# One transposing transfer for each block of four units, and fewer units turned on TensorE, in the backward loop of an attention and MLP block

## The chip, the cores and the metric

The kernel runs on one core of a Trainium2 chip. Its time is the device time of one execution in microseconds, given as the median of several runs. The engines are named as in the profile: PE is TensorE, PEld its weight load, DVE VectorE, ACT ScalarE, POOL GpSimd, SP SyncE, which here only issues DMAs.

## The reference

A transformer block with adaptive layer norm is run forward, and the gradients of its inputs and weights are computed. There are 2048 tokens, a width of 512, 32 heads of 16 columns each and an MLP of 1792 columns with a squared ReLU.

```
h = layernorm(x) * (1 + ca) + sa
x = x + ga * attention(h, wqkv, wo)
h = layernorm(x) * (1 + cb) + sb
x = x + gb * (relu(h @ w1 + b1)**2 @ w2 + b2)
out, vjp = jax.vjp(f, x, wqkv, wo, w1, b1, w2, b2, c, w_mod)
return out, *vjp(grad_out)
```

The part that matters here is the gradient of attention. With scores S = q k^T / 4, E is exp of the scores, normalised by rows; dP is the product of the output's gradient with v. Then dS = E * (dP - row sums), dV = E^T dO, dK = dS^T q and dQ = dS k. Scores and dS have 2048 x 2048 entries for each head.

## The kernel before

The kernel has three stages. The first makes the forward pass and the gradient of the MLP (to about 1116 us in the profile), the second is the backward loop of attention (to about 2388 us), and the third makes the gradients of the projections and of the norm. The change is in the second alone.

The backward loop goes over 8 groups of four heads (`hg`), four chunks of 512 keys (`kc`), four chunks of 512 queries (`qc`) and four tiles of 128 queries (`qi`). One step of the innermost loop is a *unit*: 128 queries by 512 keys for four heads. Four units with the same `hg`, `kc` and `qc` are a *block*; there are 512 units and 128 blocks. For each unit

- PE makes the scores of the four heads (`score`, L1594) into one of three PSUM banks A, B and C, and ACT takes their exponentials (`expo`, L1600) into `E_u`;
- PE makes dP for two heads at a time (`dp_pair`, L1614), and DVE multiplies by `E_u` (L1616), which gives `dS_u` in bf16, with queries on the partitions;
- PE adds `dS_u` and `E_u` into dK and dV (`k_quad` L1654, `v_quad` L1663), in one accumulator `accVK` for each chunk of keys.

dQ needs dS with the keys on the partitions. So every unit, 128 x 2048 values of 2 bytes, that is 0.5 MB, is turned into the tile `dsT`, in one of two ways. Most units are turned by a transposing DMA from SBUF to SBUF, issued by SP (`transpose_unit`, L1629 and L1631). In every second block (`on_pe`) the fourth unit is turned on TensorE instead (`pe_turn`, L1644, 16 squares of 128 x 128 in two halves into PSUM), and ACT copies the halves into `dsT` (L1760). When a block's `dsT` is whole, PE makes its dQ in 16 products (`dq_quad`, L1681) and ACT scales it out of PSUM (`dq_out`, L1691 or L1694); POOL adds it up over the chunks of keys (L1699).

`dS_u` is held in tiles of two units, of which there are four, and `dsT` in tiles of a block, of which there are three.

The order of instructions on PE, ACT, DVE, SP and POOL is written out by hand. The loop over blocks b walks through one of two lists of tokens: `order_t` in a block whose predecessor has a unit turned on TensorE, `order_n` otherwise. A token `s3` is the score 3 of the 16 of block b, `e3` its exponential, `D` the next dP pair and its dS, `q` the next dK or dV quad, `t1`, `T1`, `t2` and `T2` the two halves of the turn of block b - 1 on PE and their copies on ACT, `d1` and `d2` two dQ quads each of block b - 2, `Q` their way out, and `f`, in `order_t` alone, an extra product of PE (`keep_warm`, L1637). Both lists hold 16 scores, 16 exponentials and 8 D. The D run a little behind: the first D of block b makes the last dS of block b - 1. After a unit's second D the loop calls `transpose_unit`, so the transfers are issued by SP in the order of the units, and each waits there for its dS.

The loads of the next group of heads are issued by ACT within the loop, one for each four D. The loads of the third stage are issued by SP behind the last transfers (from L1778 on).

Of the kernel before, what the change touches and what calls it, by code (L numbers as in the profile page):

```python
# [17 lines left out]
BF = dt.bfloat16  # L18
F32 = dt.float32

P = 128
# [13 lines left out]
def kernel(  # L35
# [21 lines left out]
    SP = nc.sync  # L57
# [89 lines left out]
    with ExitStack() as ph:  # L147
# [4 lines left out]
        ework = att.enter_context(tc.tile_pool(name="phCe", bufs=4))  # L152
# [1393 lines left out]
        SP.dma_start(out=tile_ap, in_=(dQc if key == "dq" else dVKtP)[i])  # L1546

    with ExitStack() as ph:
        tpool = ph.enter_context(tc.tile_pool(name="phIt", bufs=3))
        ework = ph.enter_context(tc.tile_pool(name="phIe", bufs=4))  # L1550
        wk = ph.enter_context(tc.tile_pool(name="phIw", bufs=2))
        psd = ph.enter_context(tc.tile_pool(name="psId", bufs=2, space=bass.MemoryType.PSUM))
# [3 lines left out]
        hst, bst, sst, dqt, cur = {}, {}, {}, {}, {}  # L1556
# [45 lines left out]
        def dp_pair(u, pair):  # L1602
            hg, kc, qc, qi = units[u]
            st = hst[hg]
            qt = qc * 4 + qi
            if pair == 0:
                if qi % 2 == 0:
                    cur["dS"] = ework.tile([P, 2, 4, 512], BF, name="dS_u", tag="dS_u", bufs=4)
                bst[u][1] = cur["dS"][:, qi % 2]
            E_u, dS_u = bst[u]  # L1610
            psD = psd.tile([P, 2, 512], F32, name="psD_u", tag="pd")
            for hi in range(2):
                r = 32 * (2 * pair + hi)
                PE.matmul(psD[:, hi, :], st["do"][r:r + 32, qt * P:(qt + 1) * P], st["v"][r:r + 32, kc * 512:kc * 512 + 512],  # L1614
                          start=True, stop=True, tile_position=(r, 0))
            DVE.tensor_tensor(dS_u[:, 2 * pair:2 * pair + 2, :], psD[:], E_u[:, 2 * pair:2 * pair + 2, :], ALU.mult)  # L1616
            if qi == 3 and on_pe(u // 4):
                held["dS"] = dS_u

        def on_pe(b):  # L1620
            return b % 2 == 1

        def transpose_unit(u):
            hg, kc, qc, qi = units[u]
            if qi == 0:
                dqt[u // 4] = tpool.tile([P, 4, 16, P], BF, name="dsT", tag="dsT")
            if on_pe(u // 4) and qi >= 2:
                if qi == 2:
                    SP.dma_start(out=dqt[u // 4][:, qi], in_=bst[u][1].rearrange("p h k -> p (h k)"), transpose=True)  # L1629
            elif qi % 2 == 1:  # L1630
                SP.dma_start(out=dqt[u // 4][:, qi - 1:qi + 1].rearrange("p u b q -> p (u b) q"),  # L1631
                             in_=cur["dS"].rearrange("p u h k -> p (u h k)"), transpose=True)

        held = {}

# [84 lines left out]
        with tc.manual_schedule(engines={PE.engine, ACT.engine, DVE.engine, SP.engine, POOL.engine}):  # L1720
# [3 lines left out]
            idle = psx.tile([P, 512], F32, name="idle", tag="accVK")  # L1724
            for b in range(NU // 4 + 3):
                toks, bank = order_t if on_pe(b - 1) else order_n
                for tok in toks:
                    c, i = tok[0], int(tok[1:] or 0)
# [11 lines left out]
                    elif c == "D":  # L1740
                        if 0 <= nD < 2 * NU:
                            dp_pair(nD // 2, nD % 2)
                            if nD % 2 == 1:
                                transpose_unit(nD // 2)
                        nD += 1
                        cur["j"] = nD
                        for j in sorted(j for j in todo if j <= nD):
                            for f, args in todo.pop(j):
                                f(*args)
                    elif c == "q":  # L1750
                        if 0 <= nq < 2 * NU:
                            (v_quad if nq % 2 else k_quad)(nq // 2)
                        nq += 1
                    elif c == "f" and 0 < nq < 2 * NU:
                        keep_warm()
                    elif c == "t" and 0 <= b - 1 < NU // 4:
                        pe_turn(b - 1, i - 1)
                    elif c == "T" and 0 <= b - 1 < NU // 4:
                        dst, pt = held.pop(i - 1)
                        ACT.activation(dst, pt[:], AF.Identity)  # L1760
                    elif c == "d" and 0 <= b - 2 < NU // 4:
                        for kt in (2 * i - 2, 2 * i - 1):
                            dq_quad(b - 2, kt)
                    elif c == "Q" and 0 <= b - 2 < NU // 4:
                        dq_out(b - 2)
# [3 lines left out]
    with ExitStack() as ph:  # L1769
# [139 lines left out]
        with tc.manual_schedule(engines={PE.engine, ACT.engine, DVE.engine}):  # L1909
# [33 lines left out]
            for b in range(3):  # L1943
                for ic in range(DC):
# [8 lines left out]
                    elif i <= 2 * DC:  # L1953
                        k, h = (i - 1) // 2, (i - 1) % 2
# [67 lines left out]
```

## Time and profile before

| | |
|---|---|
| median of three runs | 2492.1 us (2487.35 to 2492.11) |
| profiled execution, from its first to its last instruction | 2501.3 us |
| busy: PE, DVE, ACT, POOL | 93%, 73%, 92%, 20% of the span |
| mean granted clock of TensorE | 0.98 |
| backward loop | 1115.7 to 2387.6 us |
| DMA packets | 1189503, of which 1065867 under 512 B |

The profiled execution is one run by itself, with the profiler on; the page gives no other time for it than its span. Busy shares are means over three stages with different limits: in the first stage DVE is busy half of the time, in the loop almost all of it. A row of a timeline has its start in us, its length, engine, line, operation, output and input, and in brackets the idle time before it and what ended that. A row of the chain has start, length and what the chain ran over.

### The profile page before, as it was taken

To read this page: it belongs to the slowest core of one execution; us is meant where nothing else is said; L and a number is where in the kernel's file an instruction comes from. 1 tells how busy PE (TensorE), PEld (TensorE's weight loads), DVE (VectorE), ACT (ScalarE), POOL (GpSimd) and SP (SyncE) were. 2 spreads that over 40 slices of the span, in tenths; PEclk is the share of its full clock that TensorE was granted. 3 is DMA by queue.
4 is the path that set the end of the run, shared out by engine and by line. 5 is a ranking of instruction groups with operands and counts; after the bars stand their busy time and mean duration, and the time that the engine had idled before them with its cause. 6 is when DMAs were issued, how large, how long until landed. Compare 5 with 4: busy or idle time off the path is not lost.

```text
span 2501.3 us, 49888 instructions
## 1 busy us (share of the span) xinstructions
PE 2324.0 (93%) x18948; PEld 783.4 (31%) x19036; DVE 1837.7 (73%) x2377; ACT 2303.7 (92%) x3560; POOL 488.0 (20%) x661
## 2 busy tenths in 40 slices
PE   8899899989998998999999999999999999999989
PEld 3232233223332333443223323233232323332344
DVE  6555354455435444579989999999999999999965
ACT  7999999999998999539999999999999999999944
POOL 2111223323533453110111101111011110110100
PEclk9999999999998999999999999999999999999999
DMA  4468463258546865979999999999999999999984
GB/s 146 130 167 176 144 150 97 88 166 142 98 95 142 151 131 110 256 200 196 201 192 206 199 198 202 196 204 203 205 205 198 205 202 199 200 198 214 201 253 133
DMA packets 1189503, 437.70 MB, mean 175 GB/s; under 512 B 1065867, under 2 KB 1160521, under 8 KB 1188878
## 3 DMA queue, kind: packets, MB, share of 16 engines
q1 hardware_dynamic: 1152414, 389.35, 79.0%
q0 software_dynamic: 19872, 27.09, 6.5%
q10 hardware_dynamic: 16976, 18.07, 2.9%
q8 instruction: 149, 2.44, 0.4%
q14 instruction: 92, 0.75, 0.1%
HBM read 98.30 MB, written 70.80 MB: 68 GB/s over the span
## 4 chain that ended last, share of the span: by engine, by line
ACT 40%; PE 38%; issue 8%; DVE 7%; DMA 3%; SPq 1%; ACTq 1%; POOL 0%; DVEq 0%; another core or an unknown queue 0%; POOLq 0%
ACT E_u L1600 24%; ACT ET L578 12%; PE dqacc L1681 4%; PE psST L576 3%; PE psS_A L1594 3%; PE accVK L1654 2%; PE pm L233 2%; ACT dsT L1760 2%; PE psS_B L1594 2%; PE pdh L1858 2%; PE oacc L592 2%; PE psS_C L1594 2%; PE pwq L1892 2%; PE pm L500 2%; PE pm L410 2%
## 5 line engine op out<-in xcount | busy, mean ns | idle before, releaser
L1616 DVE TENSOR_TENSOR dS_u<-psD_u,E_u 128x1024 bf16<-128x1024 f32 x1024 | 1185.9, 1218 | 77.1 <-PE psD_u L1614 30.2
L578 ACT ACTIVATE ET<-psST 128x1024 bf16<-128x1024 f32 x1024 | 941.9, 1242 | 16.6 <-PE psST L576 16.3
L1600 ACT ACTIVATE E_u<-psS_A 128x512 bf16<-128x512 f32 x768 | 509.9, 664 | 10.8 <-PE psS_C L1594 8.5
L1600 ACT ACTIVATE E_u<-psS_B 128x512 bf16<-128x512 f32 x768 | 503.2, 655 | 10.8 <-DMA dsT<-dS_u 2.7
L1614 PE MATMUL psD_u<-iv,ido 32*128 32x512 bf16 x2048 | 409.1, 388 | 1.5 <-DVE dS_u L1616 1.3
L576 PE MATMUL psST<-qt_sb,kt_sb 32*128 32x512 bf16 x2048 | 313.8, 386 | 48.0 <-ACT ET L578 41.0
L1600 ACT ACTIVATE E_u<-psS_C 128x512 bf16<-128x512 f32 x512 | 334.3, 653 | 3.1 <-PE psS_B L1594 1.1
L1594 PE MATMUL psS_B<-ik,iq 32*128 32x512 bf16 x768 | 296.1, 386 | 11.7 <-ACT E_u L1600 4.4
L1594 PE MATMUL psS_A<-ik,iq 32*128 32x512 bf16 x768 | 294.5, 383 | 11.0 <-DVE dwlast L237 1.0
L1699 POOL TENSOR_TENSOR dQacc<-dQacc,dqtmp 128x512 f32<-128x512 f32 x64 | 81.2, 1268 | 858.8 <-ACT dqtmp L1694 797.4
L1594 PEld LDWEIGHTS <-iq 32*128 32x128 bf16 x2048 | 129.7, 91 | 313.9 <-issue 296.9
L1654 PE MATMUL accVK<-dS_u,qz 128*32 128x512 bf16 x2048 | 213.5, 388 | 0.5 <-PE psD_u L1614 0.2
L592 PE MATMUL oacc<-ET,vaug 128*32 128x512 bf16 x2048 | 207.0, 394 | 3.9 <-DVE ostage L596 3.9
L1663 PE MATMUL accVK<-E_u,dOs_tok 128*16 128x512 bf16 x2048 | 204.5, 388 | 0.0
L1594 PE MATMUL psS_C<-ik,iq 32*128 32x512 bf16 x512 | 194.2, 379 | 4.5
L576 PEld LDWEIGHTS <-kt_sb 32*128 32x128 bf16 x2048 | 84.3, 91 | 328.2 <-issue 306.5
L1681 PE MATMUL dqacc<-dsT,KS_tok 128*32 128x512 bf16 x2048 | 145.7, 382 | 18.8 <-DMA dsT<-dS_u 5.0
L1760 ACT ACTIVATE dsT<-ptT 128x1024 bf16<-128x1024 bf16 x128 | 144.1, 1126 | 13.1 <-PE ptT L1644 12.2
L251 DVE COPY part<-pm 128x512 f32<-128x512 f32 (+2 forms) x106 | 65.2, 615 | 121.9 <-PE pm L233 111.8
L1614 PEld LDWEIGHTS <-ido 32*128 32x128 bf16 x2048 | 105.2, 91 | 101.3 <-issue 94.9
L1654 PEld LDWEIGHTS <-qz 128*32 128x32 bf16 x2048 | 58.5, 94 | 178.0 <-issue 162.9
L1699 POOL TENSOR_TENSOR dQst<-dQacc,dqtmp 128x512 bf16<-128x512 f32 x32 | 40.6, 1270 | 266.1 <-ACT dqtmp L1694 266.1
(415 smaller groups left out, 2688.7 us busy)
## 6 DMA issues: line engine op xcount, KB each, us to landing
p_st<-part POOLq DMA_DIRECT2D x36, 256.0 KB, 4.6
kt_sb<-qkT_st POOLq DMA_DIRECT2D x124, 64.0 KB, 3.0
wA<-in_B_w_dram SPq DMA_DIRECT2D x28, 256.0 KB
wB<-w1T_st SPq DMA_DIRECT2D x21, 256.0 KB
wA<-w2T_st SPq DMA_DIRECT2D x21, 256.0 KB
wB<-in_B_w_dram SPq DMA_DIRECT2D x21, 256.0 KB
p_st<-part POOLq DMA_DIRECT2D x28, 192.0 KB, 4.6
p_st<-part SPq DMA_DIRECT2D x18, 256.0 KB
```

Source lines behind the costliest of these rows:

```text
L576: PE.matmul(ps[:, hi, :], kt_sb[r:r + 32, kt * P:(kt + 1) * P], qt_sb[r:r + 32, :], start=True, stop=True, tile_position=(r, 0))
L578: ACT.activation(ET[:, 2 * pair:2 * pair + 2, :], ps[:], AF.Exp, scale=SCALE)
L592: PE.matmul(oacc[32 * hq:32 * hq + 32, :], lhsT, ET[:, hq, :], start=(kt == 0), stop=(kt == TT - 1), tile_position=(0, 32 * hq), skip_grou ...
L1594: PE.matmul(psS[:], st["q"][r:r + 32, qt * P:(qt + 1) * P], st["k"][r:r + 32, kc * 512:kc * 512 + 512], start=True, stop=True, tile_positi ...
L1600: ACT.activation(bst[u][0][:, hq, :], sst.pop((u, hq))[:], AF.Exp, scale=SCALE)
L1614: PE.matmul(psD[:, hi, :], st["do"][r:r + 32, qt * P:(qt + 1) * P], st["v"][r:r + 32, kc * 512:kc * 512 + 512], start=True, stop=True, til ...
L1616: DVE.tensor_tensor(dS_u[:, 2 * pair:2 * pair + 2, :], psD[:], E_u[:, 2 * pair:2 * pair + 2, :], ALU.mult)
L1654: PE.matmul(cur["vk"][32 * hq:32 * hq + 32, :], hst[hg]["qz"][:, qt, hq, :], bst[u][1][:, hq, :], start=(qt == 0), stop=False, tile_positi ...
L1663: PE.matmul(acc[32 * hq:32 * hq + DH, :], dOs_tok[:, qt, (hg * 4 + hq) * DH:(hg * 4 + hq + 1) * DH], E_u[:, hq, :], start=False, stop=(qt ...
L1681: PE.matmul(acc[32 * hq:32 * hq + 32, :], KS_tok[:, kc * 4 + kt, h * DH:h * DH + 32], tT[:, :, hq * 4 + kt, :], start=(kt == 0), stop=(kt ...
L1699: POOL.tensor_tensor(dst2, dst, tmp[:], ALU.add)
L1760: ACT.activation(dst, pt[:], AF.Identity)
```

## The change

A dS tile now holds the four units of a block, and three such tiles are there instead of four of two units. The block is turned by one transfer, issued when its last unit to be turned by DMA is there: four units, or three in a block whose fourth is turned on TensorE. TensorE turns the fourth unit of every fourth block instead of every second. `dsT` has two tiles instead of three. `order_t` is now walked through in every fourth block, `order_n` in the others. The lists themselves, and all else, stay as they are; from there on the lines of the file move up by three (L1631 becomes L1628, L1681 becomes L1678, L1760 becomes L1757).

```diff
-        tpool = ph.enter_context(tc.tile_pool(name="phIt", bufs=3))
+        tpool = ph.enter_context(tc.tile_pool(name="phIt", bufs=2))
...
             if pair == 0:
-                if qi % 2 == 0:
-                    cur["dS"] = ework.tile([P, 2, 4, 512], BF, name="dS_u", tag="dS_u", bufs=4)
-                bst[u][1] = cur["dS"][:, qi % 2]
+                if qi == 0:
+                    cur["dS"] = ework.tile([P, 4, 4, 512], BF, name="dS_u", tag="dS_u", bufs=3)
+                bst[u][1] = cur["dS"][:, qi]
...
         def on_pe(b):
-            return b % 2 == 1
+            return b % 4 == 1
 
         def transpose_unit(u):
             hg, kc, qc, qi = units[u]
-            if qi == 0:
+            w = 3 if on_pe(u // 4) else 4
+            if qi == w - 1:
                 dqt[u // 4] = tpool.tile([P, 4, 16, P], BF, name="dsT", tag="dsT")
-            if on_pe(u // 4) and qi >= 2:
-                if qi == 2:
-                    SP.dma_start(out=dqt[u // 4][:, qi], in_=bst[u][1].rearrange("p h k -> p (h k)"), transpose=True)
-            elif qi % 2 == 1:
-                SP.dma_start(out=dqt[u // 4][:, qi - 1:qi + 1].rearrange("p u b q -> p (u b) q"),
-                             in_=cur["dS"].rearrange("p u h k -> p (u h k)"), transpose=True)
+                SP.dma_start(out=dqt[u // 4][:, 0:w].rearrange("p u b q -> p (u b) q"),
+                             in_=cur["dS"][:, 0:w].rearrange("p u h k -> p (u h k)"), transpose=True)
```

## The prediction

> **What bounds the kernel now.** I read the page first, then the loop alone in the windows view, then the transfers of dsT, the chain, the timelines of SP, ACT and DVE, and the loop's end.
>
> The window of the backward loop, whose columns are its length, then busy time of PE, PEld, DVE, ACT and POOL, then granted clock, DMA share (over 1 where queues overlap) and GB/s:
>
> ```profile
> 1115.70:2387.60 1271.90, 1218.51 (x11551) 379.64 (x11550) 1185.88 (x1024) 1230.14 (x2335) 148.01 (x107) 0.98 1.16 200
> ```
>
> ACT is busy 97%, DVE 93%, and the DMA engines carry the transposes almost without a break. So three resources lie within a few per cent of each other, and taking work from one shows only what the next allows. The two kinds of transfer and the eviction of the TensorE turn (minimum, median, maximum ns):
>
> ```profile
> L1631 SPq DMA_TRANSPOSE dsT<-dS_u x192: 4766/5266/6831, 1123.7 to 2377.1; - x192
> L1760 ACT ACTIVATE dsT<-ptT x128: 1023/1162/1167, 1140.7 to 2379.4; 128x1024 bf16<-128x1024 bf16 x128
> L1629 SPq DMA_TRANSPOSE dsT<-dS_u x64: 1759/2336/4402, 1140.0 to 2382.1; - x64
> ```
>
> The SP queue in a stretch of the loop: the three transfers of two units and the one of one unit fill 18.8 of 19.4 us, and the queue hardly rests:
>
> ```profile
> 1499.59 2.08 SPq L1629 DMA_TRANSPOSE dsT<-dS_u  x1
> 1503.39 16.67 SPq L1631 DMA_TRANSPOSE dsT<-dS_u  x3
> 1520.15 2.17 SPq L1629 DMA_TRANSPOSE dsT<-dS_u  x1
> 1522.77 16.77 SPq L1631 DMA_TRANSPOSE dsT<-dS_u  x3
> ```
>
> The DMA view of 1499.6 to 1538.4, one digit and one rate for each 0.97 us: rates of 290 while a transfer runs freely, 215 in other stretches, and a hole about once in one and a half transfers:
>
> ```profile
> DMA  9999099999949999099999999903999999999999
> GB/s 291 282 224 191 0 168 261 130 214 250 119 123 176 290 290 207 8 243 224 218 217 219 234 192 232 172 0 69 304 187 94 280 280 148 290 289 291 259 217 217
> ```
>
> First exponentials of three blocks in a row; between them lie 16 exponentials each, so the block without a TensorE turn (call it N) takes 8.61 us and the one with it (T) 10.84:
>
> ```profile
> 1506.95 0.60 ACT L1600 ACTIVATE E_u<-psS_C 128x512 bf16<-128x512 f32 x1
> ...
> 1515.56 0.66 ACT L1600 ACTIVATE E_u<-psS_A 128x512 bf16<-128x512 f32 x1
> ...
> 1526.40 0.60 ACT L1600 ACTIVATE E_u<-psS_C 128x512 bf16<-128x512 f32 x1
> ```
>
> The chain of waits through the dQ products that use dsT, and DVE's row: 16 products in a run, 1.167 us each:
>
> ```profile
> 1503.12 1.07 PE dqacc L1681 x16
> 1510.63 0.62 PE dqacc L1681 x8
> 1522.52 1.05 PE dqacc L1681 x16
> 1529.99 0.61 PE dqacc L1681 x8
> ```
>
> ```profile
> 1505.20 18.67 DVE L1616 TENSOR_TENSOR dS_u<-psD_u,E_u 128x1024 bf16<-128x1024 f32 x16 [0.71 <-PE accVK L1663]
> ```
>
> From 1200 to 2300 us the dQ products wait 0.3 us for a transfer, all told, so the chain runs over ACT and PE. That transfers are near the limit shows in one place, where ACT's queue stood 2.7 us behind one.
>
> **Part 1: half of the TensorE turns go.** 64 of 128 evictions and 512 of 1024 PE transposes go, with the f tokens (keep_warm). 64 x 1.126 us (mean) = 72 us of ACT. By block: before, four blocks are T N T N = 2 x (10.84 + 8.61) = 38.9 us; after, N N T N = 36.7. That would give 2.2 x 32 = 72 us if nothing else were late. DVE is next: 32 products x 1.167 = 37.3 us in four blocks, so 1.6 x 32 = 51 us is the most that I grant.
>
> **Part 2: the transfers carry 15 units instead of 14 in four blocks.** At 5.266/2 = 2.63 us a unit that is 39.5 us, over what the blocks would take; it is less if part of a transfer's time is paid once. That part is not a row of its own. The holes in the rates, some 0.6 us for each transfer, are its nearest row; nothing (one long transfer is just two) is the other end. A four-unit transfer, W, is 2 x 5.27 = 10.5 without any saving; with one handover saved 9.9 to 10.0; with all of it at 290 GB/s, which no stretch keeps up, 2.1 MB/290 = 7.2. The end below is taken as 9.0 (233 GB/s, between the two rates). I take 10.0, the value nearest to the measured transfers. The order of the changed program confirms 96 transfers of 64 squares of 128x128 and 32 of 48, so the change does what it says.
>
> **Part 3: the whole block lands at its end.** Before, half of a block was on its way while the other half was made. Now it starts when the last dS is written. In the SP rows the issue at 1503.39, after a rest, marks the second unit of a block ready; four more products of DVE (4 x 1.17 and 0.7 idle) put the fourth at 1508.7, that is 1.9 us before the dQ products of the N block at 1510.63. Those of the next N block would stand 8.6 us later, so a transfer has 10.5 us. It needs 1.2 us to its first data (after the issue at 1503.39 the queue's data begins at about 1504.5), W = 10.0, and some 0.75 until PE can go on. For this last I use the loop's end:
>
> ```profile
> 2373.49 4.61 DVE L1616 TENSOR_TENSOR dS_u<-psD_u,E_u 128x1024 bf16<-128x1024 f32 x4
> ...
> 2382.07 1.93 SPq L1629 DMA_TRANSPOSE dsT<-dS_u  x1
> ...
> 2386.60 1.17 PE L1681 MATMUL dqacc<-dsT,KS_tok 128*32 128x512 bf16 x16 [4.35 <-DMA dsT<-dS_u]
> ```
>
> Issue to use is 4.5 us for one unit: 1.2 + 2.6 of data + 0.75. So 11.95 us is needed and 10.5 is there: PE waits 1.45 us at the quads of the T block's own transfer (index 2 of four). The next transfer (index 3) starts right behind it and ends 10.0 later, where the N block allows 8.6: another 1.4. Index 0 is used in a T block, whose quads come some 3.4 us later into the block, and index 1 carries three units (about 7.6 us): both land in time and let the queue catch up. Behind the waiting product on PE are the scores, so ACT and DVE stand still too; the two waits add to the period.
>
> The period, closed as a loop: from the quads of one N block to the last dS of the T block behind it 19.36 - 1.9 = 17.4 us (rows of the chain), then 1.2 + 2 x 10.0 + 0.75 to the quads again: 39.35 us. Before, the typical four blocks are 2 x 19.36 = 38.7, and the mean over the loop, from the first SP issue of 1123.7 to that of 2377.1, is 1253.4 us/127 x 4 = 39.5. The 0.8 between typical and mean are disturbances (head loads issued by ACT, clock drops); half of them should fall into time that now waits for the transfer anyway, so I add 0.35: 39.7. Difference +0.2 x 32 = +6 us.
>
> **Part 4: the end.** Block 127 is no longer turned on TensorE. Before, the last quads start at 2386.60, 8.5 us after the last dS (2378.10). After, with 126 and 127 in the queue, 1.2 + 20.0 + 0.75 = 21.95 from the last dS of 126, less a block of 8.6: 13.3. That is +4.8 us, exposed, since the last loads of SP and all of the phase behind follow.
>
> **At no cost:** three dS tiles of four units instead of four of two, and two dsT tiles instead of three. A transfer waits for the one two blocks earlier, which lands a block before; a dS tile waits for the one three back. If that cover went, the loss would be a share of 8.6 us a block. ACT's head loads wait for an earlier transfer on their semaphore, the nearest 2.2 blocks old, once in each head; 0 to 1.4 us each, 0 to 10 us in all, taken as 0. POOL waits for ACT before and after.
>
> **Sum.** -72 of ACT's work, all of it turned into waits for transfers: +6 in the loop, +5 at the end, +11. The profiled execution spans 2501.3 us, 9.2 above the median 2492.1; the sum is a difference, so I put it on the median: 2503. About 0.2% (5 us) is what a measurement can tell here.
>
> **Rivals.**
> *Long transfers are cheaper.* If W is below 9.8, 39.35 falls by 0.2 for each 0.1 and the sign turns; at 9.4 it gives 38.15 + 0.35 = 38.5, -1.0 x 32 + 4 = -28; at 9.0 and below DVE's 37.3 + 0.6 holds it: -1.6 x 32 + 4 = -47. So 2445 to 2475, likeliest 2464. For it: 290 GB/s in many stretches. Against: two units are already 1 MB, and the 215 stretches lie in mid-transfer. The Trainium skill (DMA: Bandwidth & Descriptors, Rules for kernel authors) says to coalesce small transfers and that those under 64 KB pay mostly overhead; these are far above, and the one-unit row agrees that little is fixed (2.34 against 5.27). Chance 0.31.
> *Clock drops.* Each wait may let TensorE's clock fall, as at the loop's end behind the idle 4.35 us, and in mid-loop for 3.4 us:
>
> ```profile
> 1476.00:1479.40 3.40, 3.40 (x21) 1.08 (x20) 2.86 (x3) 2.93 (x5) 0.00 (x0) 0.50 1.15 213
> 2387.40:2390.80 3.40, 3.40 (x38) 3.10 (x31) 2.07 (x4) 2.15 (x3) 1.27 (x1) 0.50 1.01 375
> ```
>
> A T block with a drop is 1.2 us longer (its evictions 3.1 apart, else 1.9). In half of 64 waits: +38 more, 2541. The Trainium skill (TensorE: Matmul & The Clock Gate, Part 1) asks for an idle window of about 3.4 us; by that rule waits of 1.45 do nothing, though the drop at 1476 came without such an idle. Chance 0.12.
> *No saving at all in W* (10.5): +1.0 x 32 = +32, 2535. Chance 0.14.
> *Forecast:* W 9.8 to 10.2, 2490 to 2520. Chance 0.43.
>
> **Chances and range.** Faster: the first rival and a little of the forecast, 0.34. Within 0.2%: the forecast's lower edge, 0.13. Slower: 0.53. Range 2452 to 2540.
>
> **What would show it.** Right: DMA waits of dqacc in mid-loop, two in four blocks of 1 to 2 us, SP transfers near 10 us, ACT's busy time down by some 70 us with the loop no shorter. Wrong: SP times below 9.5, dqacc never waiting, and DVE's row without idle; or dS_u or ACT waiting for a transfer instead.

## The result: 2652.9 us, 6.5% slower, and the profile after

The changed kernel takes 2652.9 us (median of four runs, 2646.8 to 2654.2), the kernel before 2491.7 us (2487.4 to 2492.1): 1.0652 times as long, interval 1.0631 to 1.0673. The prediction had the direction right, at 2503 us, and the size far wrong.

The profiled execution spans 2650.0 us, 148.7 more than before. From the first exponential of the loop to its last dS it is 1406.1 us (1118.8 to 2524.9) where it was 1262.4 (1115.7 to 2378.1). So 143.7 us came into the loop and 7.7 into the stretch from the last dS to the end of the last dQ quads (17.4 us, before 9.7). The rest of the kernel was 2.7 us shorter.

The same window of the loop as the prediction showed, with the same columns:

```profile
1115.70:2545.00 1429.30, 1249.08 (x10951) 338.42 (x10950) 1197.31 (x1033) 1197.29 (x2274) 149.75 (x108) 0.86 1.07 192
```

ACT is busy 84% of this window where it was 97%, DVE 84% where it was 93%, and the DMA share fell from 1.16 to 1.07. None of the three close resources is the limit any more. The clock, third number from the end, went from 0.98 to 0.86: the records show 396 us of the loop at half clock, before 58.

The transfers (tile view, minimum, median and maximum in ns) and the waits from 1200 to 2400 us, with their sum, number and longest:

```profile
L1628 SPq DMA_TRANSPOSE dsT<-dS_u x128: 7208/9728/11709, 1133.1 to 2527.3; - x128
L1757 ACT ACTIVATE dsT<-ptT x64: 1024/1143/1162, 1151.2 to 2507.9; 128x1024 bf16<-128x1024 bf16 x64
```

```profile
DVE dS_u L1616 <- PE psD_u L1614: 130.7, 121, 4.3
ACT E_u L1600 <- PE psD_u L1614: 95.3, 115, 4.0
...
PEld L1678 <- DMA dsT<-dS_u: 84.0, 40, 4.5
...
PE dqacc L1678 <- DMA dsT<-dS_u: 55.7, 31, 3.9
PE psS_C L1594 <- ACT E_u L1600: 48.0, 55, 2.0
...
ACT E_u L1600 <- PE psS_B L1594: 27.0, 55, 0.7
```

The first row mixes two lengths: the 96 transfers of four units take 9.87 us in the median, near the 10.0 that was forecast, the 32 of three units 7.61. The dQ products wait for them, as forecast. The first two rows of waits have grown: DVE and ACT mostly wait for PE's dP products, where in the kernel before (1200 to 2300 us) these two waits came to 24.0 and 1.2 us. The pair at the end has grown as well: ACT waits for a score in bank B, before 1.3 us, and PE for bank C, a wait that was not there before.

One N block with its successor shows how these hang together. PE's timeline has the time idle and what ended it in brackets:

```profile
1607.66 0.37 PE L1594 MATMUL psS_C<-ik,iq 32*128 32x512 bf16 x1 [0.75 <-ACT E_u L1600]
...
1613.24 0.99 PE L1678 MATMUL dqacc<-dsT,KS_tok 128*32 128x512 bf16 x8 [1.71 <-DMA dsT<-dS_u]
1614.16 0.60 PE L1594 MATMUL psS_B<-ik,iq 32*128 32x512 bf16 x1
...
1619.84 0.37 PE L1594 MATMUL psS_C<-ik,iq 32*128 32x512 bf16 x1 [0.75 <-ACT E_u L1600]
```

```profile
1606.60:1610.00 3.40, 2.53 (x28) 0.73 (x26) 3.40 (x4) 2.94 (x8) 0.00 (x0) 1.00 1.27 274
1610.00:1613.40 3.40, 1.69 (x16) 0.33 (x16) 2.87 (x3) 3.07 (x7) 0.00 (x0) 0.99 1.27 210
1613.40:1616.80 3.40, 3.40 (x31) 0.61 (x23) 1.22 (x1) 1.25 (x3) 0.27 (x1) 0.51 1.19 231
1616.80:1620.20 3.40, 2.65 (x28) 0.80 (x28) 3.31 (x3) 2.98 (x6) 1.00 (x1) 1.00 1.17 217
1620.20:1623.60 3.40, 3.40 (x25) 0.46 (x21) 2.80 (x4) 2.90 (x6) 0.00 (x0) 0.50 0.95 159
1623.60:1627.00 3.40, 3.40 (x24) 0.61 (x27) 2.41 (x3) 2.13 (x5) 0.00 (x0) 0.50 1.14 227
1627.00:1630.40 3.40, 3.40 (x28) 0.68 (x20) 2.64 (x3) 2.65 (x6) 1.27 (x1) 0.50 1.16 218
```

PE waits 1.71 us for the transfer. In the 3.4 us up to 1613.4 it begins 16 products and is busy for half of the time, and from then on the clock is 0.5: a score takes 0.60 us where it took 0.37. At 1616.8 the clock is back. From 1620.2 it is 0.5 again for three windows, and this second drop follows no wait for a transfer: PE's longest idle in the window before is 0.75 us, for bank C. In the three windows PE is busy all the time and begins 24 to 28 products in each, where an N block before had 78 in 8.6 us, 31 in 3.4; ACT and DVE wait for it. By whole blocks, each from its first exponential:

```profile
1608.10:1620.20 12.10, 9.52 (x84) 2.17 (x80) 9.31 (x9) 9.21 (x18) 1.27 (x1) 0.86 1.22 226
1620.20:1631.80 11.60, 11.56 (x86) 2.05 (x82) 9.25 (x9) 9.09 (x17) 1.27 (x1) 0.56 1.09 203
1631.80:1642.40 10.60, 10.11 (x107) 3.68 (x110) 9.64 (x9) 10.45 (x21) 1.27 (x1) 1.00 0.88 164
```

The second N block (11.60 us) waits for no transfer and is slow by the clock alone: without a drop such a block takes 8.54 us. In blocks 8 to 119 there are 28 such second blocks; 23 of them wait for no transfer, and their length follows the time at half clock almost exactly, 8.57 us and 0.31 us more for each us at half clock (a line through the 23, correlation 0.99). The T block is what it was (10.60), and in it the clock has come back.

Over blocks 8 to 119 the four blocks of a cycle (transfers of index 0 to 3 in the prediction's count) last in the mean 12.7, 10.6, 10.9 and 9.6 us. Those in which no drop falls have a median of 9.82, 8.54, 10.63 and 9.18, sum 38.2, though only 3 and 9 of 28 blocks of the first two kinds are such. The quiet sum before was 10.80 + 8.54 + 10.64 + 8.54 = 38.5. So the change does save ACT's work, and a little of that shows in the blocks that keep the clock.

### The profile page after: what moved, and what is told of

Its sections match the earlier page's. It is cut to its first block, busy times and chain, and to the rows that moved or that the text cites. A ratio compares the mean times of both kernels' runs of the same rounds, so it can differ in the third digit from the quotient of the medians.

```text
span 2650.0 us, 47994 instructions
## 1 busy us (share of the span) xinstructions
PE 2351.1 (89%) x18307; PEld 739.6 (28%) x18395; DVE 1845.0 (70%) x2377; ACT 2268.1 (86%) x3496; POOL 489.0 (18%) x661
## 4 chain that ended last, share of the span: by engine, by line
PE 37%; ACT 26%; DMA 21%; issue 7%; DVE 7%; ACTq 1%; POOL 0%; SPq 0%; another core or an unknown queue 0%; DVEq 0%; POOLq 0%
DMA dsT<-dS_u 19%; ACT E_u L1600 12%; ACT ET L578 12%; PE dqacc L1678 5%; PE psST L576 3%; PE psS_A L1594 3%; PE psS_B L1594 2%; PE accVK L1651 2%; PE pm L233 2%; PE psS_C L1594 2%; PE oacc L592 2%; PE accVK L1660 2%; PE pwq L1889 2%; PE pdh L1855 2%; PE pm L500 2%
## 5 line engine op out<-in xcount | busy, mean ns | idle before, releaser
L1600 ACT ACTIVATE E_u<-psS_B 128x512 bf16<-128x512 f32 x768 | 479.0, 624 | 117.3 <-PE psD_u L1614 96.6
L1600 ACT ACTIVATE E_u<-psS_A 128x512 bf16<-128x512 f32 x704 | 443.5, 630 | 27.7 <-PE psD_u L1614 16.4
L1614 PE MATMUL psD_u<-iv,ido 32*128 32x512 bf16 x2048 | 444.1, 430 | 0.4 <-DVE dS_u L1616 0.4
L1600 ACT ACTIVATE E_u<-psS_C 128x512 bf16<-128x512 f32 x576 | 360.1, 625 | 41.3 <-PE psS_B L1594 30.2
L1594 PE MATMUL psS_B<-ik,iq 32*128 32x512 bf16 x768 | 330.0, 430 | 19.9 <-ACT E_u L1600 9.8
L1594 PE MATMUL psS_C<-ik,iq 32*128 32x512 bf16 x576 | 237.6, 413 | 56.1 <-ACT E_u L1600 53.1
L1678 PE MATMUL dqacc<-dsT,KS_tok 128*32 128x512 bf16 x2048 | 192.9, 473 | 89.5 <-DMA dsT<-dS_u 77.0
L1651 PE MATMUL accVK<-dS_u,qz 128*32 128x512 bf16 x2048 | 235.7, 437 | 1.1 <-DVE dS_u L1616 0.9
L1660 PE MATMUL accVK<-E_u,dOs_tok 128*16 128x512 bf16 x2048 | 220.2, 419 | 0.0
L1678 PEld LDWEIGHTS <-KS_tok 128*32 128x32 bf16 x2048 | 43.2, 99 | 193.2 <-DMA dsT<-dS_u 107.2
```

What stands on the lines that cost most here:

```text
L1594: PE.matmul(psS[:], st["q"][r:r + 32, qt * P:(qt + 1) * P], st["k"][r:r + 32, kc * 512:kc * 512 + 512], start=True, stop=True, tile_positi ...
L1600: ACT.activation(bst[u][0][:, hq, :], sst.pop((u, hq))[:], AF.Exp, scale=SCALE)
L1651: PE.matmul(cur["vk"][32 * hq:32 * hq + 32, :], hst[hg]["qz"][:, qt, hq, :], bst[u][1][:, hq, :], start=(qt == 0), stop=False, tile_positi ...
L1660: PE.matmul(acc[32 * hq:32 * hq + DH, :], dOs_tok[:, qt, (hg * 4 + hq) * DH:(hg * 4 + hq + 1) * DH], E_u[:, hq, :], start=False, stop=(qt ...
L1678: PE.matmul(acc[32 * hq:32 * hq + 32, :], KS_tok[:, kc * 4 + kt, h * DH:h * DH + 32], tT[:, :, hq * 4 + kt, :], start=(kt == 0), stop=(kt ...
```

## The experiments

The chip was asked three things: which part of the change costs what, whether the clock or the waits carry the loss, and what makes the clock fall. "Half clock" is the sum of the time at half clock in the loop of the profiled execution, and "cycle" the median and mean of four blocks in it (blocks 8 to 119). The kernel before, run beside them, took 2487.2 to 2489.4 us.

| kernel | us | ratio (95%) | half clock, us | cycle, us | idle of dqacc for transfers, us |
|---|---|---|---|---|---|
| before | 2491.7 | 1 | 58 | 38.94 / 39.38 | 5 |
| after | 2652.9 | 1.0652 (1.0631 to 1.0673) | 396 | 43.89 / 43.86 | 77 |
| e1_pe_part | 2566.8 | 1.0309 (1.0287 to 1.0331) | 256 | 41.60 / 41.25 | 21 |
| e2_merge_part | 2530.0 | 1.0169 (1.0146 to 1.0191) | 82 | 39.38 / 40.47 | 25 |
| e3_banks | 2637.3 | 1.0574 (1.0534 to 1.0614) | 348 | 43.27 / 43.54 | 114 |
| e4_warm | 2667.2 | 1.0713 (1.0692 to 1.0735) | 212 | 44.59 / 44.42 | 16 |
| e7_warm4 | 2654.1 | 1.0677 (1.0633 to 1.0721) | 352 | 44.03 / 44.25 | 22 |
| e5_late_banks | 2600.4 | 1.0452 (1.0427 to 1.0478) | 256 | 41.50 / 42.04 | 34 |
| e6_late | 2719.3 | | 765 | 46.11 / 46.00 | 11 |
| e8_pe_late_banks | 2570.7 | 1.0334 (1.0304 to 1.0365) | 222 | 41.00 / 41.29 | 15 |
| e9_late_fill | 2590.8 | 1.0409 (1.0354 to 1.0463) | 106 | 40.50 / 42.17 | 15 |
| e10_fill | 2662.2 | 1.0744 (1.0670 to 1.0817) | 167 | 43.15 / 43.57 | 49 |
| e11_before_no_f | 2524.4 | 1.0149 (1.0113 to 1.0185) | 154 | 40.79 / 40.11 | 2 |
| e12_pe_late_fill3 | 2562.6 | 1.0287 (1.0262 to 1.0312) | 109 | 39.30 / 41.24 | 16 |

(The runs of e6 lay between 2670 and 2732 us, too far apart for a ratio; its trace is of the longest. Even the shortest, 2670 us, had a mean granted clock of 0.888 over the whole execution, where the runs of after had 0.912 to 0.916.) Of the last column 2 to 11 us lie at the loop's end, behind the last block: 4 before, 10 after.

### The two parts, each alone

e1 is the kernel before with fewer TensorE turns and its own two-unit transfers; e2 is the changed kernel with a turn in every second block.

```diff
 # e1, in the kernel before
-            return b % 2 == 1
+            return b % 4 == 1
 # e2, in the kernel after
-            return b % 4 == 1
+            return b % 2 == 1
```

> One part alone: one unit in sixteen on TensorE, but the transfers stay as they were, of two units each (and of one unit in a block with a turned unit). Theory 1 (the late landing of whole blocks makes PE wait, and the wait drops TensorE's clock): the last two units of a block need 1.2 + 5.3 + 0.75 = 7.3 us and 10.5 are there, so the first wait is gone; the queue still has 15 x 2.63 = 39.5 us of work in four blocks, so short waits stay. Time 2490 to 2560, granted clock of the loop over 0.93. Rival A (the queue's total work is the bound, whatever the size): about as slow as the whole change, 2600 to 2650. Rival B (the loss is the bank that two blocks without a turn share at their border, 0.64 us at two borders in four blocks): 2492 + 41 - some 40 of ACT's work = 2490 to 2530, with no DMA waits.

> The other part alone: one transfer for each block, with one unit in eight on TensorE as before. Theory 1: every four-unit transfer is then used in a block with a turn, whose quads come 3.4 us later, so that 14 us are there and 11.95 needed; the three-unit one has 14.4. No waits in mid-loop, clock as before, time 2485 to 2505 and mostly the same as before. Rival A (a long transfer is bad in itself, or the queue's work bounds): over 2550. Rival B (bank at the border): no two blocks without a turn follow each other, so 2480 to 2500 as well.

Each part alone is slower: fewer turns by 78 us, long transfers by 41. Together they cost 161, 42 more than the sum. The half clock goes with the first part: 256 us in e1, and 82 in e2, little over before. The windows from 1115.7 to 2400 us of e1 and then e2:

```profile
1115.70:2400.00 1284.30, 1158.27 (x10491) 322.18 (x10486) 1148.43 (x990) 1148.42 (x2192) 138.42 (x100) 0.90 1.17 203
```

```profile
1115.70:2400.00 1284.30, 1206.86 (x11400) 371.00 (x11399) 1178.20 (x1015) 1217.80 (x2314) 141.71 (x103) 0.97 1.11 195
```

In e1 the transfers are those of before and the dQ products wait 12 us for them ahead of the loop's end, yet the cycle is 1.9 us longer in the mean. What has changed is PE's run of work: in blocks 8 to 119 its idle times of over 0.15 us add up to 89 us, 77 of them for ACT, where before they came to 7. So the turns that were taken away had held something up that no row of ACT shows. In e2 the transfers make PE wait 19 us ahead of the loop's end (1 before), and ACT's queue, which issues the loads of the next heads, waits for a transfer for 7.8 us where that was 2.7:

```profile
ACT E_u L1600 <- DMA dsT<-dS_u: 7.8, 2, 4.1
```

With some 7 us for 24 us more at half clock (at 0.3, priced below) that is 30 of the 34 us that e2's loop is longer, if every wait counts in full. By place most of it is not where the forecast had its waits: the seven cycles that begin a group of heads take 43.4 us in the mean where they took 40.0, which is 24 of the 31 us that blocks 8 to 119 are longer. The other 21 cycles take 39.5 us where they took 39.2. In each of the seven ACT stands for 1.5 to 4.1 us in the third or fourth block; in two of them the trace names a DMA as the cause, in the others that is not shown.

### The border of the banks

In two N blocks in a row the last score of the first and the first score of the second are both made in bank C. That is seen above at 1607.66: PE waits 0.75 us for ACT. Before, an N block was always followed by a T block, and this border did not exist. e3 gives such blocks another list of banks:

```diff
                 toks, bank = order_t if on_pe(b - 1) else order_n
+                if not on_pe(b - 1) and not on_pe(b):
+                    bank = "CBACBACBABABACBA"
```

> The whole change, but in a block without a turn that is followed by another the last scores go to banks A B A C B A, so that the next block's first score does not ask for the bank of the last one. Rival B (the border costs 0.64 us, twice in four blocks): 2652 - 41 = 2611. Theory 1: the wait for the transfer takes up what the first border gives; 2611 to 2652, and the granted clock stays at 0.86.

The fourth block falls from a median of 9.18 us to 8.65, as it should if this is the border's price of 0.64 (9.18 less 8.54). The time falls by only 16 us, where 0.64 x 2 x 32 = 41 were to be had: the dQ products now come earlier and wait longer, 114 us where it was 77. The border is real and is mostly hidden behind the transfer.

### Is it the wait that drops the clock?

e4 and e7 put extra products (128x128x512, into a bank that the first quad overwrites) ahead of the dQ products that wait, eight and four of them.

```diff
             tT = dqt[b]
+            if kt == 0 and b % 4 >= 2:
+                for _ in range(8):    # e7: 4
+                    PE.matmul(acc[:], ones_bf[:], dOs_tok[:, 0, :], start=True, stop=True, skip_group_check=True)
```

> The whole change, with eight extra products of PE into the dQ bank (overwritten by the quads) ahead of the first dQ quad of the blocks with index 2 and 3 of four, that is in the time that PE waits for the transfer. Theory 1 with the clock as the larger part of the loss: the clock stays near 1.0, the waits remain or are filled, and the time falls from 2652 to 2530 to 2580. Rival C (the waits alone make the loss, the clock is only their mark): no gain, or slower by up to 64 x 1.7 = 110 us where the products are in the way.

> The whole change with four extra products instead of eight ahead of the late quads (0.86 us instead of 1.72; the wait at full clock is 1.1 to 1.7). Theory 1: the filler takes less than the wait it fills, so the half-clock time lies between that of no filler (396 us) and of eight (212), and the time below both, 2600 to 2650. Rival C (the waits alone): 2652 as with none.

With eight products the idle time goes from 77 to 16 us and the half clock from 396 to 212 us; with four, to 22 and 352. The time doesn't fall. The trace says why: e4's extra products keep PE busy for 155 us, more than the waits that they fill. In the trace of after 25 of the 47 drops behind the first two blocks have a wait for a transfer in the 3.4 us ahead of them. So such a wait is one way to a drop. But e7 waits almost as little as e4 and keeps nine tenths of the half clock: what held the clock in e4 may be the added work, not the missing wait. Either way, bridging the wait with work is no remedy.

### Quads later, with the banks in turn and without

e5 moves the dQ quads and their way out to a later place in `order_n`, so that the transfer has some 2.4 us more, and gives both successions of blocks banks without a border. e6 has the same order of work and leaves the border between N blocks. e8 is e5's lists with the transfers of before, that is e1 with both remedies.

```diff
-            "e5 s6 q s7 D s8 e6 e7 d1 e8 s9 D d2 e9 q Q s10 "
-            "s11 e10 D q s12 e11 e12 s13 e13 D q s14 s15 e14 e15 D q ").split(), "CBACBACBABABCABC"
+            "e5 s6 q s7 D s8 e6 e7 e8 s9 D e9 q s10 "
+            "s11 e10 D q s12 e11 d1 e12 s13 D d2 e13 q Q s14 s15 e14 e15 D q ").split(), "CBACBACBACBABABC"
...
+                if not on_pe(b - 1) and not on_pe(b):       # not in e6
+                    bank = "CBACBACBACBABABA"
```

> The whole change, with the dQ quads and their way out moved some three microseconds later in the blocks without a turn (behind exponential 11 instead of 7), and the banks of the scores set so that no first score asks for the bank of the last one. Theory 1 (the wait for the transfer, and the clock that falls behind it): the transfers have 13.4 us instead of 10.5, the waits go, the clock of the loop returns to 0.96 or more and the period falls from 43.9 to 38.2 (the transfers' own 10.0 + 8.1 + 10.4 + 9.7) to 39: 2450 to 2490, level with the kernel before or better. Rival A (long transfers are bad in themselves): still over 2580.

> The same later quads, with the banks at the border of two blocks without a turn left in conflict. Theory 1 with the border as a cost of its own: 0.6 us at two borders in four blocks, so up to 38 us above the run with the banks set, less what the transfers' 38.2 us hide. Rival B (the border is the main loss): most of the 160 us would still be there, over 2580.

> Transfers of two units as before, one unit in sixteen on TensorE, and the later quads and set banks. Theory 1: the last half of a block lands 7.3 us after its last dS, the waits go as well; the period is then the queue's 15 x 2.63 = 39.5 or the engines' 37.3, whichever the queue allows: 2450 to 2500. If long transfers save anything, this is slower than the run with one transfer for a block.

e5 is 52 us faster than the changed kernel, with the waits at 34 us. But half clock remains at 256 us, and e8, in which hardly a product waits for a transfer (15 us, 11 of them at the loop's end), still has 222. e6 is the sharpest case. Ahead of the loop's end PE waits for a transfer once, for 0.4 us, and its clock is by far the worst:

```profile
1115.70:2400.00 1284.30, 1215.58 (x9358) 310.12 (x9356) 1038.12 (x887) 1051.05 (x1960) 129.35 (x92) 0.75 1.05 181
```

```profile
PE psS_C L1594 <- ACT E_u L1600: 29.8, 73, 0.8
...
PE dqacc L1678 <- DMA dsT<-dS_u: 0.4, 1, 0.4
```

Here PE's short waits of at most 0.8 us, many in a row, go with 765 us at half clock, and some stretches last over 30 us. In the 3.4 us ahead of 39 of its 40 drops PE has no idle over 0.7 us. So long idle times are not needed. In the kernel before, 12 of 13 drops even have no idle over 0.2 us ahead of them, with PE busy for 97% of that time by the profile.

Where the drops begin says more. In before, where N and T blocks alternate, all 13 begin in T blocks. In after 42 of 47, in e1 25 of 30 and in e8 22 of 34 begin in an N block that follows another N block. I counted PE's matmul records in the 3.4 us before each drop and in 3.4 us stretches without one, in before, after, e5 and e8: 17 to 24 in the median before a drop and at most 28, 29 to 32 in the median otherwise. The two overlap (some stretches with 18 to 24 kept the clock), and some records can be missing from a trace, so this is a tendency and not a threshold.

### Extra products that hold the clock

If sparse work drops the clock, then PE can hold it with work that nobody needs. e9 is e5 with one extra product ahead of the scores 3, 5, 7, 9 and 11 of N blocks (into the bank that the score overwrites), e10 is e3 with the same five, e12 is e8 with three (scores 3, 7 and 11). e11 goes the other way: it takes the `f` tokens, products of this kind, out of the kernel before.

```diff
             sst[u, hq] = psS
+            if not on_pe(u // 4 - 1) and (4 * qi + hq) in (3, 5, 7, 9, 11):    # e12: (3, 7, 11)
+                PE.matmul(psS[:], ones_bf[:], dOs_tok[:, 0, :], start=True, stop=True)
 # e11
-                    elif c == "f" and 0 < nq < 2 * NU:
-                        keep_warm()
```

> The run with later quads and set banks, with one extra product of PE (128x128 by 512, overwritten by the score) ahead of scores 3, 5, 7, 9 and 11 of the blocks without a turn. That run waits little for transfers and yet shows 256 us at half clock. Theory 2 (what drops the clock is PE's sparse work in blocks without a turn that follow each other, a wait for a transfer being only one way to it): the five products lift the number of products in a window of 3.4 us, the half-clock time falls below 120 us and the period from 42.0 to 38.5 to 40, 2480 to 2540 against 2600. Theory 1 (only the wait for a transfer drops the clock): the clock stays as it is, and the products add up to 96 x 1.07 = 103 us where PE is the bound: 2600 to 2700.

> The whole change with set banks and the quads where they were, with the same five extra products. Theory 2: fewer drops than the 348 us without them, but the transfer still lands late, and PE's wait of 1 to 2 us leaves a sparse window: 2560 to 2630 against 2637. Theory 1: as many drops as without, 2637 to 2740.

> The kernel before without the f tokens, the extra products that stand in blocks with a turn alone (they add zeros). Theory 2: they hold the clock up in those blocks; without them the half-clock time of the loop rises from 58 us to over 150, and the time from 2489 to over 2520. If the work around a turn is dense enough by itself: no change, or up to 64 x 4 x 0.2 = 55 us less where PE is the bound.

> e8 (the transfers of before, every fourth block turned on TensorE, dQ quads later, banks in turn) with three extra products of 128x128x512 in each block of order_n, ahead of scores 3, 7 and 11. Theory (sparse products of PE cost the clock, and each extra product costs PE its own time): the time at half clock falls from 222 us to 100 to 170, the N blocks without a drop go from 9.0-9.4 to 9.3-9.6, and the time is 2545 to 2580, still slower than before. Rival (the saved turns pay as soon as transfers and clock are no longer in the way, three products being cheap): 2460 to 2490. Other rival (three products do not reach the density that holds the clock): half-clock time still 200 or more, time 2575 to 2600.

In e9 the half clock falls from 256 to 106 us, and of 8 drops one lies in an N block. But an N block without a drop is now 9.6 to 9.95 us (e5: 9.0 to 9.4), and the time falls by 10 us only, less than e9's own runs differ (2574 to 2603). e10 has 181 us less at half clock than e3 and takes 25 us more. e11 loses 37 us: the `f` products of the kernel before earn their place. Its trace is of its shortest run, 30 us over before, and has 96 us more at half clock:

```profile
1115.70:2400.00 1284.30, 1187.19 (x11219) 363.14 (x11220) 1185.99 (x1023) 1227.70 (x2327) 143.43 (x104) 0.94 1.13 197
```

Behind the first two blocks it has 42 drops, and all begin in T blocks, where the `f` were; no N block has one. No dQ product of the loop waits for a transfer, and PE has no idle over 0.6 us ahead of any drop. A T block takes 11.9 us with a drop and 10.6 to 10.8 without, 0.32 to 0.37 us for each us at half clock. Nothing else was changed, so this run shows that taking work from PE is enough to drop the clock. e12 has the lowest time of the variants with fewer turns, though its interval overlaps with e1's and e8's. Its median cycle is 39.30 us, 0.36 over before, and its half clock 109 us; the mean cycle is 41.24. That excess lies mostly at one place, the border between two groups of heads, where ACT issues the loads of the next: the cycle there is 45.7 us in the mean; the others take 39.3, but for one of 48.4 at 1251 us that has no such stop. Rows of ACT's queue and of ACT, and two windows show it:

```profile
1643.04 0.35 ACTq L1576 DMA_DIRECT2D iqs<-q_st  x1
1648.62 0.33 ACTq L1576 DMA_DIRECT2D dQc<-dQst  x1
1649.05 0.60 ACT L1602 ACTIVATE E_u<-psS_A 128x512 bf16<-128x512 f32 x1 [5.42 <-DMA iqs<-q_st]
```

```profile
1645.20:1648.60 3.40, 0.00 (x0) 0.00 (x0) 0.00 (x0) 0.00 (x0) 0.00 (x0) 0.96 1.20 127
1648.60:1652.00 3.40, 2.30 (x17) 0.36 (x20) 1.28 (x2) 2.24 (x5) 0.00 (x0) 0.50 1.16 216
```

ACT's queue stands 5.4 us at its next DMA, all engines stop, and the clock falls for some 10 us.

The expectations of these runs can be read against the table. Theory 1, by which the clock comes back when the waits for transfers go, gave times that were missed by far in e4 (2530 to 2580), e5 (2450 to 2490), e6 (38 us above e5 at most) and e8 (2450 to 2500), and by less in e1, e2 and e7; only e3 came out within its range. The theory of sparse work had the half clock right in e9, e11 and e12, and the time in e11 and e12; e9 and e10 took longer than it said. No variant was faster than the kernel before, and none of what was seen points to one.

## Why the prediction was wrong

**What held.** The direction came out right, but with luck: it had a chance of 0.53, and of the +11 us none was for what became the largest loss. The change does what it says. A four-unit transfer takes 9.87 us in the median where I took 10.0, and the evictions fell from 144.1 to 72.0 us in all, the 72 us worked out. ACT's busy time fell by only half of that, from 2303.7 to 2268.1 us, so this sign of the forecast's list was badly chosen: exponentials in a run start 0.48 us apart and last 0.6, so they overlap, and when ACT waits between them each counts in full. Part 3 had one of the two places of the waits: of the 77 us that dqacc is idle for transfers 56.5 lie in the first N block, 26 waits with a median of 2.15 us, where 1.45 was worked out. In the second N block, where I had 1.4 each time, there are only 5 waits, 8.3 us in all, and 9.7 us lie at the end. In four blocks that makes 2.1 us, for my 2.85. DVE's 37.3 us never became the limit. The rival of long transfers that are cheaper is refuted: W, at 9.87, is not below the 9.8 from which it would have decided.

**The step that failed: the rival "Clock drops", its chance (0.12) and its count.** I let a drop come in half of 64 waits, 3.4 us each, 32 x 1.2 us = 38 us. The price of a drop was near the measured one, its number was not. The loop has 338 us more at half clock, which is 99 stretches of 3.4 us. At my 1.2 us for each that is 119 us of the 143.7. Three other prices lie close together: 0.31 us for each us at half clock in the second N blocks that wait for no transfer, 0.32 to 0.37 in the T blocks of e11, and 0.29 between executions of the same kernel, which differ in their mean clock (a line through all runs of after and e1 to e12, each taken from the mean of its kernel; in e10, 2659 us at a clock of 0.961 and 2695 at 0.939). The length of a whole cycle over its time at half clock gives 0.23 (after) to 0.52 (e2, e12), but there waits and drops come together. By these three prices the 338 us are some 100 to 125 us. So the clock is the largest part of what the loop lost, and the forecast's sum had no term for it.

Why I set it aside: by the rule of the Trainium skill (TensorE: Matmul & The Clock Gate, Part 1) an idle window of some 3.4 us is needed, and my waits were 1.45. The trace disagrees: 1.71 us idle at 1611.5 are followed by half clock at 1613.4, and e6 drops with idle times below 0.7. The prediction itself had shown a drop in mid-loop without such an idle, and that row should have decided. The section "A second HAM failure mode: psum-queue depth-cycling" on the same page of the Trainium skill describes the case better, a clock that goes to and fro because PE is idle for many short times between groups of products; e6's border of the banks agrees, with 73 waits of 29.8 us in all. The drops of the kernel before, with no idle over 0.2 us ahead of them, it does not explain.

**Part 1 looked at ACT only.** Two N blocks in a row are the stretch in which the clock falls, even where hardly a transfer is waited for (e8, 222 us). It is not that an N block has fewer products for its length: the lists hold 80 products for N and 100 for T, over 8.54 and some 10.8 us, 9.4 and 9.3 in each us. What grew is PE's idle time within the blocks (7 us before, 89 in e1, 125 in after, of which 60 for transfers and 65 for ACT). I counted the turns as work that is saved, and `f` as gone with them, and never asked what they held up.

**A missed term: the border of the banks.** N behind N did not exist in the trace of before, and its list of banks begins and ends with C. In quiet blocks it is 0.64 us, twice in four blocks: 1.3 x 32 = 41 us at most, of which e3 got back 16.

**The period.** I had 39.7, and 43.9 was measured. Counted from blocks that lose nothing, three N blocks of 8.54 and a T block of 10.63 make 36.3 us. The 12.2 us at half clock in a cycle add 3.8 at 0.31, the two borders 1.3, and PE's waits for transfers 2.1 (60 us in 28 cycles): 43.5, and 0.4 stays unexplained. So the clock is about half of the 7.6 us that a cycle loses. The split is an estimate: e3 shows that a border and a wait hide each other in part, and a wait also drops the clock.

**Part 4** gave +4.8 us for the end; it is +7.7. The last two transfers took 10.3 and 11.2 us for my 10.0, and the last dQ products, at half clock, wait twice:

```profile
2527.80 1.90 PE L1678 MATMUL dqacc<-dsT,KS_tok 128*32 128x512 bf16 x16 [1.84 <-DMA dsT<-dS_u]
...
2540.36 1.90 PE L1678 MATMUL dqacc<-dsT,KS_tok 128*32 128x512 bf16 x16 [7.88 <-DMA dsT<-dS_u]
```

**"At no cost"** held for the tiles. ACT's waits at head loads, 0 to 10 us by my bounds and taken as 0, are 8.0 us in two where 2.7 was: within the bounds in this kernel, and much more in e12 (24 us in six, and the clock behind them). In e2 most of the loss lies in the cycles where these loads are.

**What stays open.** What exactly the clock gate measures was not found; the count of products before a drop only leans the right way, and why the kernel before drops at all, with PE busy, is not known. How the loss divides between the clock, the waits and the border is an estimate, since no run gave the loop its clock back for nothing. Moving ACT's head loads out of reach of the transfers was not tried.

## What to carry to other kernels

Work that is taken off TensorE may have been what held its clock: before removing PE work, look at the idle times and products of the few microseconds that remain around it, not at the mean of a block, and take a drop in the trace without a long idle as a warning that the margin is used up. When a change makes a new succession of blocks, walk through the buffers across that border by hand; a trace of the old kernel cannot show it. And in a loop like this one, where several engines are near their limit, a wait on another resource can cost twice, once as time and once as the clock that falls behind it.

## What was not expected of the hardware

- Half clock lasts in steps of 3.4 us, and in this loop mostly 3.4 to 10.2 us at a time; in e6 up to 34 us. PE busy all the time, by the profile, did not bring it back at once: the windows from 1620.20 to 1630.40 have PE at 3.40 us of 3.40 and a clock of 0.50 three times in a row. The Trainium skill (TensorE: Matmul & The Clock Gate, Part 1) gives a busy window of about 3.4 us for the return; this trace disagrees.
- A wait of 1.7 us in a sparse stretch was followed by half clock, and so were idle times under 0.7 us, many in a row (e6, e11).
- A microsecond at half clock cost this loop about 0.3 us (0.29 to 0.37 by the three ways above), not a half.
- One transfer of 2 MB took 9.9 us where two of 1 MB took 10.5: uniting them saved some 6%.
